# Two feed-forward layers on one core: the first product from a 7-product scheme over 2x2x2 blocks to a 20-product scheme over 3x4x2 blocks

## The chip, the cores and the metric

The kernel runs on one core of a Trainium2 chip. The metric is device microseconds (us) of one execution, lower is better. Engines are named as the profile names them: PE (TensorE), PEld (its weight loads), DVE (VectorE), ACT (ScalarE), POOL (GpSimd), SP (SyncE, which here only issues DMAs).

## The reference

Hashed attention feeds two feed-forward layers. The change is in the layers; of the attention it touches only the last steps, which hand the layers their input.

```
attn_out = attention with a mask of equal hash buckets   # (2, 8, 768, 64)
x = attn_out.transpose(0, 2, 1, 3).reshape(1536, 512)
h = np.maximum(x @ w_in, 0.0);  x = h * h @ w_out        # layer 1, w_in 512x2048, w_out 2048x512
h = x @ w2_in;  out = (h * sigmoid(h)) @ w2_out          # layer 2, same shapes
```

The weights are drawn as float64.

## The kernel before, in words

**Exactness.** Every float32 operand of a product is split into a high part (a cast to fp32r) and a low part (operand minus high part); a product is three matmuls, high-high, high-low, low-high, into one PSUM bank. A 128x512 result with a contraction of 128 is thus three matmuls of 512 columns. Where a value is "cut" below, ACT casts the high part (L158) and DVE or POOL subtracts it (L160); both are in `split` (L156).

**Weights.** They arrive as 64-bit words by DMA, one tile of 128x512 at a time (`convert`, L165), and are rebuilt as float32 by one ACT and four DVE instructions (L173 to L177). A tile of w_in then goes into `wp`, cut on ACT and POOL, four sums of halves are formed on DVE (L215), and these are cut too (`convert_in`, L200); a tile of w_out is cut on ACT and DVE (`convert_out`, L180).

**Loops.** `moe` (L129) runs over two layers m and four ff blocks f; a block has four ff tiles of 128, in two pairs n. Of the 1536 tokens, three token blocks of 512, block 0 is multiplied plainly (`plain`, L220: 4 ff tiles x 4 K tiles x 3 = 48 matmuls, L231). Blocks 1 and 2 go through `quarters` (L253): for each pair n, seven products over two K halves stand for eight (7 x 2 x 3 = 42 matmuls, L260), with five PSUM sums on DVE (L265) and one copy out of PSUM on ACT (L274). The gate is on ACT (`gate`, L244: Relu, and Square at L249, in layer 1; Silu in layer 2), and its result is cut (`gsplit`). `second` (L321) multiplies by w_out, 12 rows of 12 matmuls (L341), and DVE copies (f = 0) or adds (f > 0) each bank into `ys` or `y0` (L352, L355, L361); the last add goes to `ts` and out by DMA. So an ff block has 48 + 84 matmuls in the first product and 144 in the second. `blocks_of_x` (L368) forms the sums of token blocks, once per layer.

**Order.** `Plan` (L53) is a list scheduler that runs when the program is built: each operation is added with its engine, a planned cost, what it reads and writes, and the plan then fixes the order in which each engine's instructions are emitted. PE keeps the order in which its work was added. An operation marked `port` is planned never to run beside a POOL operation. Buffers are handed out in turn: 8 banks, 3 raw weight tiles, 3 float32 weight tiles, 6 scratch tiles `ts`.

**End of the attention.** `wp_put`, `wp_sums`, `x_mul`, `x_put` (POOL) and `t2_t3` (DVE) prepare, among the attention's last steps, the first weights and the token blocks of layer 1.

Of the kernel before, what the change touches and what calls it, by code (L numbers as in the profile page):

```python
# [48 lines left out]
NRAW, NWT, NWO, NTS = 3, 3, 4, 6  # L49
# [3 lines left out]
class Plan:  # L53

# [4 lines left out]
    def add(self, eng, cost, fn, reads=(), writes=(), land=0.0, after=0.0, port=False):  # L63
        n = len(self.ops)
        deps = {self.writer[k] for k in (*reads, *writes) if k in self.writer}
        for k in writes:
            deps.update(self.readers.pop(k, ()))
            self.writer[k] = n
        for k in reads:
            self.readers[k].append(n)  # L70
        if eng == "PE":
            if self.last is not None:
                deps.add(self.last)
            self.last = n
        deps.discard(n)
        self.ops.append((eng, cost, fn, deps, land, after, port or eng == "POOL"))
        return n

    def gap(self, a, b):
        return self.ops[a][4] + (self.lag if self.ops[a][0] != self.ops[b][0] else 0.0)  # L80

    def order(self):
# [6 lines left out]
        for i in reversed(range(n)):  # L89
            tail[i] = ops[i][1] + max((tail[u] + self.gap(i, u) for u in users[i]), default=0.0)  # L90
        left = [len(o[3]) for o in ops]
        when = [o[5] for o in ops]
        ready = defaultdict(list)
        for i in range(n):
            if not left[i]:
                ready[ops[i][0]].append(i)
        begin, port = [0.0] * n, 0.0
        for _ in range(n):
            best = None
            for eng, todo in ready.items():  # L100
                t = self.free.get(eng, 0.0)
                for i in todo:
                    s = max(t, when[i], port if ops[i][6] else 0.0)
                    k = (s, -tail[i], i)
                    if best is None or k < best[0]:
                        best = k, eng, i
            (s, _, _), eng, i = best
            ready[eng].remove(i)
            begin[i] = s
            end = self.free[eng] = s + ops[i][1]  # L110
            if ops[i][6]:
                port = end
            for u in users[i]:
                left[u] -= 1
                when[u] = max(when[u], end + self.gap(i, u))
                if not left[u]:
                    ready[ops[u][0]].append(u)
        self.begin = begin
        return sorted(range(n), key=lambda i: (begin[i], i))

    def emit(self):
        for i in self.order():
            self.ops[i][2]()


STEPS = ("c", "b", "p2", "e", "d", "p4")


def moe(nc, t):  # L129
    mm = nc.tensor.matmul  # L130
    vec, act, gps = nc.vector, nc.scalar, nc.gpsimd
    bank, ts, gq, g0, ys, y0, wp = (t[k] for k in ("bank", "ts", "gq", "g0", "ys", "y0", "wp"))
    plan = Plan(ready={"DVE": 2.6})
    add = plan.add
    count = defaultdict(int)

# [5 lines left out]
    idle = {"bank": list(range(8)), "ts": list(range(NTS))}  # L142

    def new_bank():
        return idle["bank"].pop(0)

    def scratch():
        return idle["ts"].pop(0)

    def done(name, i):  # L150
        idle[name].append(i)

    def tt(eng, cost, op, out, a, b, reads, writes):
        add(("DVE", "POOL")[eng is gps], cost, lambda: eng.tensor_tensor(out=out(), in0=a(), in1=b(), op=op), reads, writes, port=True)

    def split(hi, lo, src, rk, hk, lk, n, pool, after=0.0):  # L156
        h, l = {512: ((0.62, 0.70), (0.62, 1.30)), 1024: ((1.05, 1.28), (1.05, 2.60))}[n][pool]
        add("ACT", h, lambda: act.copy(out=hi(), in_=src()), rk, hk, after=after)  # L158
        eng = gps if pool else vec
        add(("DVE", "POOL")[pool], l, lambda: eng.tensor_tensor(out=lo(), in0=src(), in1=hi().bitcast(F32), op=ALU.subtract), (*rk, *hk), lk, port=True)  # L160
# [4 lines left out]
    def convert(m, io, i):  # L165
        r, w = nxt("raw", NRAW), nxt("wt", NWT)
        rt, wtt = t["raw"][r], t["wt"][w]
        word = rt.bitcast(U32).rearrange("p (n two) -> p n two", two=2)
        hi, lo = word[:, :, 1], word[:, :, 0]
        wu = wtt.bitcast(U32)  # L170
        wk = [("wt", w, 0), ("wt", w, 1)]
        add("SP", 2.9, lambda: nc.sync.dma_start(out=rt, in_=t["src"][m][io][i]), (), [("raw", r)], land=2.5)
        add("ACT", 0.68, lambda: act.activation(out=wtt, in_=hi.bitcast(F32), func=AF.Abs), [("raw", r)], wk)  # L173
        add("DVE", 0.43, lambda: vec.tensor_scalar(out=wtt, in0=wtt, scalar1=W_LO, scalar2=W_HI, op0=ALU.max, op1=ALU.min), wk, wk, port=True)
        add("DVE", 0.43, lambda: vec.tensor_scalar(out=wu, in0=wu, scalar1=5, scalar2=2, op0=ALU.logical_shift_left, op1=ALU.logical_shift_right), wk, wk, port=True)
        add("DVE", 0.70, lambda: vec.scalar_tensor_tensor(out=wu, in0=hi, scalar=0xC0000000, in1=wu, op0=ALU.bitwise_and, op1=ALU.bitwise_or), [("raw", r), *wk], wk, port=True)
        add("DVE", 0.70, lambda: vec.scalar_tensor_tensor(out=wu, in0=lo, scalar=29, in1=wu, op0=ALU.logical_shift_right, op1=ALU.bitwise_or), [("raw", r), *wk], wk, port=True)  # L177
        return w

    def convert_out(m, f):  # L180
        for i in range(FB):
            s = slot[m, f * FB + i] = nxt("wo", NWO)
            if (m, f) == (0, 0) and i < WB:
                r, w = nxt("raw", NRAW), nxt("wt", NWT)
                for cost, fn in t["first"][i]:
                    add("DVE", cost, fn, [("raw", r)], [("wt", w, 0), ("wt", w, 1)], port=True)
            else:
                w = convert(m, 1, f * FB + i)
            hi, lo = t["wo"][s]
            split(lambda h=hi: h, lambda x=lo: x, lambda w=w: t["wt"][w], [("wt", w, 0), ("wt", w, 1)], [("woh", s)], [("wol", s)], 512, False)  # L190

    def put(pb, w, op):
        a = wp[pb]
        src = t["wt"][w].rearrange("p (a b) -> p a b", a=2)
        split(
            lambda: a[:, 0, op : op + 2], lambda: a[:, 1, op : op + 2], lambda: src,
            [("wt", w, 0), ("wt", w, 1)], [("wp", pb, 0, op + k) for k in range(2)], [("wp", pb, 1, op + k) for k in range(2)], 512, True,
        )

    def convert_in(m, f):  # L200
        for n in range(NP):
            pb = n
            w = []
            for h in range(2):
                w.append(convert(m, 0, f * FB + 2 * n + h))
                put(pb, w[h], 2 * h)
            t0, t1 = (t["wt"][x].rearrange("p (a b) -> p a b", a=2) for x in w)
            k = [[("wt", x, j) for j in range(2)] for x in w]
            for out, a, b, op, ko, ka, kb in (
                (t1[:, 1], t1[:, 0], t1[:, 1], ALU.add, k[1][1], k[1][0], k[1][1]),  # L210
                (t1[:, 0], t0[:, 0], t1[:, 0], ALU.subtract, k[1][0], k[0][0], k[1][0]),
# [913 lines left out]
```

## Time and profile before

| | before |
|---|---|
| median of 3 runs (lowest to highest) | 740.61 us (740.59 to 741.18) |
| span of the profiled execution, first to last instruction | 739.4 us |
| instructions | 10895 |
| busy: PE, PEld, DVE, ACT, POOL | 99%, 85%, 83%, 62%, 34% |

The profile gives the profiled execution no other time of its own than its span; the median of the runs is 1.2 us above it. PE and PEld overlap. A matmul's record is longer than the distance to the next one, since matmuls are pipelined; a stretch divided by its number of matmuls gives the pace.

### The profile page before, as it was taken

Reading aid. Unit: us, or ns where it says so; the run is one execution under the profiler, and the core shown is the slowest. Engines: PE = TensorE matmul, PEld = TensorE weight load, DVE = VectorE, ACT = ScalarE, POOL = GpSimd, SP = SyncE. Lnnn points to the kernel's source line nnn. Section 1 sums busy time; section 2 is a strip of 40 time slices with the busy share of each in tenths; the row PEclk is TensorE's granted clock in tenths of the full one; section 3 lists DMA queues with packets and bytes.
Section 4 is the critical chain, followed back from the end, with each engine's and each line's share of the span. In section 5 each row is a group of like instructions: output and inputs, shape, how many; then the busy total and the mean of one; then the engine's idle time right before and its main releaser. Section 6 shows DMA issues by size and latency. Waiting matters only on the chain.

```text
span 739.4 us, 10895 instructions
## 1 busy us (share of the span) xinstructions
PE 732.1 (99%) x3734; PEld 627.3 (85%) x3735; DVE 610.0 (83%) x1152; ACT 461.6 (62%) x866; POOL 249.6 (34%) x219
## 2 busy tenths in 40 slices
PE   8999999999999999999999999999999999999998
PEld 4799999999998888888888888888888888888887
DVE  6899999999999998887878896788888777776442
ACT  7888998998896882773566278366335525623510
POOL 7547477877674104103103103500330320230000
PEclk9999999999999999999999999999999999999999
DMA  6987787686462113311320220002133024010012
GB/s 180 210 175 151 182 186 176 154 186 148 115 157 60 57 60 111 114 59 57 114 86 24 91 86 28 29 28 87 58 99 129 30 78 150 1 58 1 1 71 100
DMA packets 27687, 71.87 MB, mean 97 GB/s; under 512 B 4208, under 2 KB 9120, under 8 KB 27632
## 3 DMA queue, kind: packets, MB, share of 16 engines
q1 hardware_dynamic: 24872, 64.52, 31.4%
q0 software_dynamic: 2160, 5.90, 3.9%
q10 hardware_dynamic: 600, 0.75, 0.4%
q8 instruction: 30, 0.49, 0.3%
q14 instruction: 25, 0.20, 0.1%
HBM read 49.80 MB, written 3.15 MB: 72 GB/s over the span
## 4 chain that ended last, share of the span: by engine, by line
PE 95%; DVE 2%; DMA 2%; ACT 1%; issue 0%; SPq 0%; DVEq 0%; ACTq 0%
PE bank L341 35%; PE bank L260 21%; PE bank L231 12%; PE s L741 8%; PE t L777 8%; PE o L802 4%; PE o L801 4%; PE bt L534 1%; DMA fr<-in_dram 1%; PE bs L534 1%; DMA kk<-bt 1%; PE rb L831 1%; DVE tl L788 1%; DVE mt L748 1%; ACT P L761 0%
## 5 line engine op out<-in xcount | busy, mean ns | idle before, releaser
L160 POOL TENSOR_TENSOR wp<-wt,wp 128x512 fp32r<-128x512 f32 x56 | 78.2, 1407 | 329.5 <-ACT wp L158 307.5
L260 PE MATMUL bank<-xb,wp 128*128 128x512 f32 x480 | 110.1, 389 | 0.0
L788 DVE TENSOR_TENSOR tl<-t,th 128x384 fp32r<-128x384 f32 x192 | 104.8, 548 | 2.4 <-ACT th L782 2.2
L260 PEld LDWEIGHTS bank<-xb,wp 128*128 128x128 f32 x480 | 90.1, 188 | 18.7
L761 ACT ACTIVATE P<-s,mt 128x768 f32<-128x768 f32 x96 | 95.6, 996 | 10.6 <-DVE mt L753 7.1
L748 DVE TENSOR_REDUCE mt<-s 128x1 f32<-128x768 f32 x96 | 91.4, 952 | 5.5 <-PE s L741 4.9
L741 PE MATMUL s<-kk,qq 76*128 76x384 f32 (+1 forms) x384 | 84.5, 341 | 1.6 <-DMA kk<-bt 0.8
L782 ACT CAST th<-t 128x384 fp32r<-128x384 f32 x192 | 82.2, 483 | 4.0 <-PE t L777 3.4
L158 ACT CAST wp<-wt 128x512 fp32r<-128x512 f32 x56 | 34.2, 619 | 78.2 <-DVE wt L215 44.5
L231 PE MATMUL bank<-x0h,wp 128*128 128x512 f32 x256 | 80.2, 389 | 0.0
L777 PE MATMUL t<-ident,P 128*128 128x128 f32 x576 | 79.1, 272 | 1.0 <-DVE tl L788 0.9
L777 PEld LDWEIGHTS t<-ident,P 128*128 128x128 f32 x576 | 67.8, 140 | 5.7 <-DVE tl L788 1.1
L801 PE MATMUL o<-th,vv 128*128 128x384 f32 x192 | 72.5, 377 | 0.0
L741 PEld LDWEIGHTS s<-kk,qq 76*128 76x128 f32 (+1 forms) x384 | 67.8, 188 | 4.3 <-ACT P L761 2.1
L265 DVE TENSOR_TENSOR ts<-bank,ts 128x512 f32<-128x512 f32 x80 | 54.4, 690 | 19.8 <-PE bank L260 17.2
L802 PE MATMUL o<-tl,vv 128*128 128x384 f32 x192 | 64.5, 336 | 0.2 <-DVE tl L788 0.2
L245 ACT ACTIVATE ts<-bank 128x512 f32<-128x512 f32 x48 | 28.6, 596 | 49.4 <-PE bank L260 28.9
L231 PEld LDWEIGHTS bank<-x0h,wp 128*128 128x128 f32 x256 | 48.1, 188 | 9.9
L160 DVE TENSOR_TENSOR gql<-ts,gqh 128x512 fp32r<-128x512 f32 x64 | 43.8, 703 | 8.9 <-ACT gqh L158 8.9
L173 ACT ACTIVATE wt<-raw 128x512 f32<-128x512 f32 x58 | 38.1, 671 | 20.2 <-POOL wp L160 17.6
L341 PE MATMUL bank<-wol,gqh 128*128 128x512 f32 (+1 forms) x132 | 50.5, 383 | 0.0
L341 PE MATMUL bank<-woh,gql 128*128 128x512 f32 (+1 forms) x132 | 50.5, 383 | 0.0
(185 smaller groups left out, 1631.7 us busy)
## 6 DMA issues: line engine op xcount, KB each, us to landing
raw<-in_dram SPq DMA_DIRECT2D x64, 512.0 KB
kk<-in_dram POOLq DMA_DIRECT2D x15, 384.0 KB, 6.1
qq<-hq SPq DMA_DIRECT2D x28, 192.0 KB
vr<-in_dram SPq DMA_DIRECT2D x8, 384.0 KB
ta<-ob SPq DMA_DIRECT2D x31, 96.0 KB
tb<-ob SPq DMA_DIRECT2D x31, 96.0 KB
out_dram<-ts SPq DMA_DIRECT2D x11, 256.0 KB
rq<-in_dram SPq DMA_DIRECT2D x7, 384.0 KB
```

The source lines that it names most:

```text
L160: add(("DVE", "POOL")[pool], l, lambda: eng.tensor_tensor(out=lo(), in0=src(), in1=hi().bitcast(F32), op=ALU.subtract), (*rk, *hk), lk, po ...
L231: mm(bank[b], w[:, x, op, sl], t["x0"][y][:, kt], start=kt == 0 and j == 0, stop=kt == 3 and j == 2)
L260: mm(bank[b], w[:, p, op, k * 128 : k * 128 + 128], x[:, q, xop, k], start=first and k == 0 and j == 0, stop=k == 1 and j == 2, skip_group ...
L341: mm(bank[b][:, 0:wd], x, y, start=i == 0 and n == 0, stop=i == FB - 1 and n == 2)
L741: mm(s[:, n, 0:QW], t["qq"][h][0:kk, ab, c0 : c0 + 128], t["kk"][h][0:kk, ab, n * QW : (n + 1) * QW], start=ab == 0, stop=ab == 1)
L748: nc.vector.tensor_reduce(out=m[:, 0:1], in_=s[:, :, 0:QW], op=ALU.max, axis=AX.XY, negate=True)
L761: nc.scalar.activation(out=e.rearrange("p (a b) -> p a b", a=2), in_=s[:, :, 0:QW], func=AF.Exp, scale=m[:, 1:2], bias=m[:, 2:3], accum_ou ...
L777: nc.tensor.transpose(t[:, j * 128 : (j + 1) * 128], P[u, j][:, kt * 128 : (kt + 1) * 128], ident)
L782: nc.scalar.copy(out=th, in_=PT[g][0][:, 0:QW])
L788: nc.vector.tensor_tensor(out=tl, in0=t[:, 0:QW], in1=th.bitcast(F32), op=ALU.subtract)
L801: mm(o[:, 0:QW], vv, th, start=kt == 0, stop=False)
L802: mm(o[:, 0:QW], vv, tl, start=False, stop=kt == KT - 1)
```

## The change

The first product of both layers now runs over all three token blocks at once.

- In the first ff block of a layer (f = 0) it is plain for all three token blocks (3 x 48 = 144 matmuls). In the other three, `fast` multiplies, for each pair n, 3 token blocks x 4 K tiles x 2 ff tiles with 20 products of three matmuls in place of 24: 2 x 20 x 3 = 120 matmuls.
- The 20 products accumulate in chains (`CHAIN`): A and B each run on in one bank while partial results are read out between products; C and D are single products; K10, K20 and F are banks that DVE first fills ("seeds") with a sum, and on which PE then accumulates with `start=False`. Per pair n there are ten DVE instructions that read PSUM (seven into SBUF, three into another bank) and three ACT copies out of PSUM.
- Operands: eight x operands live in `xk`, twelve in `xw`; `operands()` forms them in the f = 0 block by 16 sums and 12 cuts, in place in `yf`, the one 128x4x1536 tile that holds x and later y. Weight operands: `convert_in(m, f, n)` now loads two tiles, rebuilds both with 1024-wide instructions in the one buffer `both`, forms 8 sums (one of 512, five of 256, two of 128 columns) in four groups, and cuts five groups of four 128-column tiles into `wpa` and `wpb`.
- Scratch, gate results and sums are 25 cells of 2 KB, handed out in turn (`Cell`). The 12 gate results of a block hold 24 of them until `second` is done with their token block. There are 2 raw weight tiles in place of 3.
- `second`: in layer 1 for every other row, in layer 2 for all rows but the last, ACT copies the old y into the bank first, PE accumulates on it, and DVE or ACT copies the bank out; else DVE adds as before. The order of token blocks is 1, 0, 2 (0, 1, 2 in the first block of all), and for the first of them the first two ff tiles of all four rows come before the last two. `convert_in` of the next block is added before the first and the second token block.
- `Plan` may give SBUF sums and cuts to DVE or POOL, and bank copies to DVE or ACT, whichever ends first in its plan.
- In the attention, `wp_sums`, four of eight `wp_put` and `t2_t3` go, `x_put` cuts token block 0 for four and blocks 1 and 2 for two pairs, and does one copy or sum less each.

The diff, cut to its core:

```diff
-NRAW, NWT, NWO, NTS = 3, 3, 4, 6
+NRAW, NWO, NCELL = 2, 4, 25
...
+CHAIN = {"A": (1, 2, 5, 7, 9, 15, 20), "B": (3, 4, 6, 11, 14, 16), "C": (8,), "D": (10,), "K10": (12, 18), "K20": (13, 17), "F": (19,)}
+ORDER = (8, 3, 1, 4, 2, 6, 12, 18, 11, 5, 14, 16, 7, 10, 13, 9, 17, 19, 15, 20)
+WPA = (12, 17, 6, 7, 14, 15, 11, 9)
+WPB = (18, 16, 8, 20, 13, 3, 19, 2, 4, 5, 10, 1)
+TURN = (1, 0, 2)
+SEED = [[r % 2 for r in range(NT // 128)], [1] * (NT // 128)]
...
+    EITHER = {128: (0.2, 0.45), 256: (0.35, 0.75), 512: (0.62, 1.3), 1024: (1.05, 2.6)}
...
+    def cut(hi, lo, src, rk, hk, lk, pool=True, after=0.0):
+        add("ACT", 0.62, lambda: act.copy(out=val(hi), in_=val(src)), rk, hk, after=after)
+        tt(ALU.subtract, lo, src, lambda: val(hi).bitcast(F32), 512, (*rk, *hk), lk, pool)
+
+    def psum(out, b, other, reads, writes):
+        add("DVE", 0.70, lambda: vec.tensor_tensor(out=val(out), in0=bank[b], in1=val(other), op=ALU.add), [("bank", b), *reads], writes)
...
+        for g, parts in enumerate(groups):
+            s = Cell()
+            for a, b, x, y, op in parts:
...
+                tt(op, out, x, y, 128 * (b - a), wk, [s.key])
+            o = (wpa, wpb)[g // 2][n][:, :, g % 2 * 4 : g % 2 * 4 + 4]
+            cut(o[:, 0], o[:, 1], lambda s=s: s().rearrange("p (b c) -> p b c", c=128), [s.key], [("wp", n, g, 0)], [("wp", n, g, 1)])
+            s.free()
...
+                for z, (p, q) in enumerate(((0, 0), (0, 1), (1, 0))):
+                    mm(bank[b], w[:, p], x[:, q], start=not started and z == 0, stop=z == 2, skip_group_check=started)
+
+            add("PE", 0.68, go, [*wkeys(n, r), *(("xo", r, q) for q in range(2))], [("bank", b)])
+            after(n, r, at, temp[n])
...
+        for r in order:
+            for n in range(NP):
+                product(n, r)
...
+            start = f == 0 or final or not SEED[m][r]
+            if not start:
+                add("ACT", 0.55, lambda src=src, yt=yt: act.copy(out=src, in_=yt), [yk], [("bank", b)])
...
+                fast(m, ORDER)
+            for k, c in enumerate(((0, 1, 2), TURN)[m] if f == 0 else TURN):
+                if k < NP and not (m == 1 and f == NFB - 1):
+                    convert_in(m + turn, (f + 1) % NFB, k)
+                second(m, f, c, k == 0)
...
-        def t2_t3(k):
...
```

## Rows read from the trace of the kernel before

**Rows 1.** The page: span, PE's busy time, the chain's shares by engine.

```profile
span 739.4 us, 10895 instructions
...
PE 732.1 (99%) x3734; PEld 627.3 (85%) x3735; DVE 610.0 (83%) x1152; ACT 461.6 (62%) x866; POOL 249.6 (34%) x219
...
PE 95%; DVE 2%; DMA 2%; ACT 1%; issue 0%; SPq 0%; DVEq 0%; ACTq 0%
```

**Rows 2.** The chain in order of time: start, length, work; one ff block, the end.

```profile
360.77 10.88 PE bank L231 x48
371.65 19.04 PE bank L260 x84
390.69 32.64 PE bank L341 x144
...
703.50 32.80 PE bank L341 x156
```

**Rows 3.** Stretches: us; PE, PEld, DVE, ACT, POOL busy (x instructions); PEclk; DMA; GB/s.

```profile
235.40:736.30 500.90, 500.88 (x2223) 415.21 (x2220) 386.91 (x619) 253.63 (x420) 88.66 (x61) 1.00 0.20 67
360.77:423.33 62.56, 62.56 (x278) 51.82 (x277) 50.15 (x81) 35.67 (x61) 11.21 (x8) 1.00 0.25 84
578.38:640.93 62.55, 62.55 (x277) 51.81 (x277) 47.10 (x81) 29.16 (x50) 12.81 (x10) 1.00 0.23 76
```

**Rows 4.** Instruction groups of DVE: count, busy us, mean ns of one.

```profile
L265 DVE TENSOR_TENSOR ts<-bank,ts 128x512 f32<-128x512 f32 x80 | 54.4, 690 | 19.8 <-PE bank L260 17.2
L160 DVE TENSOR_TENSOR gql<-ts,gqh 128x512 fp32r<-128x512 f32 x64 | 43.8, 703 | 8.9 <-ACT gqh L158 8.9
L215 DVE TENSOR_TENSOR wt<-wt,wt 128x256 f32<-128x256 f32 x28 | 13.2, 470 | 0.8
L176 DVE SCALAR_TENSOR_TENSOR wt<-raw,wt 128x512 uint32<-128x512 uint32 x58 | 46.9, 811 | 1.3
L177 DVE SCALAR_TENSOR_TENSOR wt<-raw,wt 128x512 uint32<-128x512 uint32 x58 | 40.6, 710 | 0.7
L174 DVE TENSOR_SCALAR wt<-wt 128x512 f32<-128x512 f32 x58 | 28.3, 487 | 2.9 <-ACT wt L173 2.8
L175 DVE TENSOR_SCALAR wt<-wt 128x512 uint32<-128x512 uint32 x58 | 27.2, 469 | 1.5
L154 DVE TENSOR_TENSOR ys<-ys 128x1024 f32<-128x1024 f32 x5 | 6.1, 1217 | 0.0
```

**Rows 5.** Instruction groups of ACT, same columns.

```profile
L158 ACT CAST wp<-wt 128x512 fp32r<-128x512 f32 x56 | 34.2, 619 | 78.2 <-DVE wt L215 44.5 <-DVE wt L177 33.8
L249 ACT ACTIVATE ts<-ts 128x512 f32<-128x512 f32 x48 | 30.3, 632 | 1.2
L274 ACT COPY ts<-bank 128x512 f32<-128x512 f32 x16 | 9.4, 586 | 11.2 <-PE bank L260 10.8
```

**Rows 6.** The low parts of the weights on POOL, same columns.

```profile
L160 POOL TENSOR_TENSOR wp<-wt,wp 128x512 fp32r<-128x512 f32 x56 | 78.2, 1407 | 329.5 <-ACT wp L158 307.5 <-issue 21.7 <-POOL wp L160 0.4
```

**Rows 7.** Timeline of DVE: start, length, instruction, idle time before it.

```profile
332.10 0.68 DVE L160 TENSOR_TENSOR gql<-ts,gqh 128x512 fp32r<-128x512 f32 x1
332.70 0.68 DVE L177 SCALAR_TENSOR_TENSOR wt<-raw,wt 128x512 uint32<-128x512 uint32 x1
333.61 0.69 DVE L355 TENSOR_TENSOR y<-bank,y 128x512 f32<-128x512 f32 x1 [0.23 <-PE bank L341]
```

**Rows 8.** Timeline of POOL about 299 us.

```profile
298.95 1.74 POOL L160 TENSOR_TENSOR wp<-wt,wp 128x512 fp32r<-128x512 f32 x1 [1.01 <-ACT wp L158]
```

**Rows 9.** Timeline of DVE about 299 us.

```profile
299.49 1.48 DVE L174 TENSOR_SCALAR wt<-wt 128x512 f32<-128x512 f32 x1
301.43 0.43 DVE L174 TENSOR_SCALAR wt<-wt 128x512 f32<-128x512 f32 x1
```

**Rows 10.** Timeline where the attention ends and the layers begin.

```profile
235.35 1.38 DVE L991 TENSOR_TENSOR ys<-ys 128x512 f32<-128x512 f32 x1
235.40 0.48 PE L231 MATMUL bank<-x0h,wp 128*128 128x512 f32 x1
```

More of the change, by code (lines that the diff above doesn't have):

```diff
@@ L140, in nxt @@
         return i
[L142 to L160, printed above, removed]
@@ new lines, in tt, with go @@
+    def tt(op, out, a, b, n, reads, writes, pool=True, after=0.0):
+        d, p = EITHER[n]
+        def go(eng):
+            ENG[eng].tensor_tensor(out=val(out), in0=val(a), in1=val(b), op=op)
+        add((("DVE", d), ("POOL", p)) if pool else "DVE", d, go if pool else partial(go, "DVE"), reads, writes, after=after, port=True)
+    def cut(hi, lo, src, rk, hk, lk, pool=True, after=0.0):
+        add("ACT", 0.62, lambda: act.copy(out=val(hi), in_=val(src)), rk, hk, after=after)
+        tt(ALU.subtract, lo, src, lambda: val(hi).bitcast(F32), 512, (*rk, *hk), lk, pool)
@@ L190, in convert_out @@
[L190 to L197, printed above, removed]
-        )
@@ L200, in convert_in @@
[L200 to L211, printed above, removed]
-                (t0[:, 0], t1[:, 1], t0[:, 0], ALU.subtract, k[0][0], k[1][1], k[0][0]),
-                (t0[:, 1], t0[:, 1], t0[:, 0], ALU.subtract, k[0][1], k[0][1], k[0][0]),
-            ):
-                add("DVE", 0.45, lambda out=out, a=a, b=b, op=op: vec.tensor_tensor(out=out, in0=a, in1=b, op=op), [ka, kb], [ko], port=True)
-            for h in range(2):
-                put(pb, w[h], 4 + 2 * h)
@@ new lines, in wkeys, with xo, block, gate @@
+    def wkeys(n, r):
+        part, i = WAT[r]
+        return [("wp", n, 2 * part + i // 4, x) for x in range(2)]
+    def xo(r):
+        part, i = XAT[r]
+        return (xk, xw)[part][:, :, i]
+    def block(i, j):
+        return yf[:, j, i * CH : (i + 1) * CH]
+    gs = {}
+    def gate(m, n, c, b=None, cell=None):
+        g = cell or Cell()
+        src, key = (g, g.key) if b is None else (lambda: bank[b], ("bank", b))
+        add("ACT", 0.62, lambda: act.activation(out=g(), in_=src(), func=AF.Silu if m else AF.Relu), [key], [g.key])
+        if m == 0:
+            add("ACT", 0.63, lambda: act.activation(out=g(), in_=g(), func=AF.Square), [g.key], [g.key])
+        hi, lo = gs[n, c] = Cell(F32R), Cell(F32R)
+        cut(hi, lo, g, [g.key], [hi.key], [lo.key])
+        g.free()
@@ new lines, in second, with x_cut, single, x_op @@
+        for z in ((0, 2), (2, 4)) if split else ((0, 4),):
+            for part, finish in jobs:
+                for i in range(*z):
+                    part(i)
+                if z[1] == FB:
+                    finish()
+    def x_cut(r, src, key, after=0.0):
+        x = xo(r)
+        cut(x[:, 0], x[:, 1], src, [key], [("xo", r, 0)], [("xo", r, 1)], after=after)
+    def single(i, j, after=0.0):
+        x_cut(AT[i, j], block(i, j), ("yf", i, j), after)
+    def x_op(out, a, op, b):
+        tt(ALU.add if op == "+" else ALU.subtract, block(*out), block(*a), block(*b), 512, [("yf", *a), ("yf", *b)], [("yf", *out)])
```

577 lines of the change are left out of this document (291 added, 286 removed).

## The prediction

> **What bounds the kernel now.** I read the page first: PE is busy for 732.1 of 739.4 us, and 95% of the chain that ended last is PE [rows 1]. Whether PE waits inside the layers is seen in the stretches: from the first product of layer 1 to the last matmul of layer 2 it is busy for 500.88 of 500.90 us, at a granted clock of 1.00, 2.4 GHz [rows 3]. The chain in order of time says what a matmul costs there: 48 in 10.88 us, 84 in 19.04, 144 in 32.64, all 0.2267 us each [rows 2]. So an ff block is 276 matmuls and 62.56 us, nothing else is on the path, and the end is 3.1 us after the last matmul (703.50 + 32.80 to 739.4) [rows 1, 2]. Beside PE, DVE is the fullest engine: 50.15 of 62.56 us in a block of layer 1, 47.10 in one of layer 2; ACT and POOL have room [rows 3].
>
> **What goes from PE.** The first product falls from 8 x 132 = 1056 matmuls to 2 x 144 + 6 x 120 = 1008; the second product keeps its number. 48 x 0.2267 = **10.9 us** less, if PE never waits. By blocks: +2.7 us in the two f = 0 blocks (65.3 us), -2.7 in the other six (59.84 us).
>
> **What comes onto DVE.** I count a block with f > 0 of layer 1 by record lengths [rows 4]. First the block of before, as a test: 8 weight tiles x (0.487 + 0.469 + 0.811 + 0.710 = 2.48) = 19.8; 8 half sums x 0.47 = 3.8; 16 low parts x 0.70 = 11.2; 10 sums and 12 adds out of PSUM x 0.69 = 15.2; together 50.0, against 50.15 in [rows 3]. Now the changed block. Four w_out tiles: 9.9. Two pairs of w_in tiles, 1024 wide: a 1024-wide operation took 1.217, or 1.73 times the 0.70 of a 512-wide one, so 2 x 1.73 x 2.48 = 8.6 (bounds 8.6 and 9.9, twice as long). Sums of weights per pair: 0.70 + 5 x 0.47, and two of 128 columns, unseen, between half of 0.47 and all of it, I take 0.33: 3.7, for two pairs 7.4. Low parts: 4 + 10 + 12 = 26 x 0.70 = 18.3, if all stay on DVE (the ten of w_in were on POOL). Out of PSUM: 20 x 0.69 = 13.8, and 6 adds 4.1. The six of these that write another bank have no row; nearest are 0.69 and, above, the longest 512-wide one, 0.81; I take 0.69. Together **62.1 us** against PE's 59.84; in layer 2, with no adds and the copies on ACT, 57.9.
>
> The records overstate it: in [rows 7] DVE starts a 0.68 instruction 0.60 after the one before. By that pace, 0.88 of the records, the block needs 54.7 us (91% of PE's time) in layer 1 and 51.0 (85%) in layer 2. I go by the pace, since it is what a full queue does. In an f = 0 block the count is 18.5 for weights, 7.4 sums, 18.3 low parts and 28 operations for the operands (19.6): 63.8 of 65.3 by records, 56.1 by pace.
>
> **What POOL can take.** In [rows 8, 9] a DVE instruction of 0.43 us that starts while POOL subtracts lasts 1.48, to 0.28 after POOL's end: 1.05 us lost for one POOL operation. A low part handed over frees 0.70 on DVE and costs POOL 1.41 [rows 6], so it relieves DVE only while DVE works out of PSUM. The Trainium skill (SBUF — State Buffer, "SBUF: two separate sides") says the same: the port pair that DVE and GpSimd share is locked for a whole instruction and the loser blocks. By that rule, with which the 1.48 agrees, handing work over does not shrink the 62.1; without it, six low parts on POOL would bring it under 59.84.
>
> **ACT and the rest.** Per block ACT gets four more copies out of PSUM (0.59), two more cuts (0.62), 6 to 12 bank seeds and as many copies [rows 5]. Writing PSUM has no row; between 0.59 and 0.62, I take 0.6. That makes some 46 us in either layer, under 59.84: hidden. Two raw tiles in place of three: the loads of one pair begin when the other has been rebuilt, and run beside its sums; hidden, else they lengthen the weights' path below. In f = 0, y may overwrite `yf` only after the operands have read it, but eight banks let `second` run 8 x 2.72 = 21.8 us without a copy, so the operands' 19.6 us have 32.6 + 21.8: hidden. Where the attention ends, the first product starts at 235.40, 0.05 after a `t2_t3` instruction that goes on for 1.38 [rows 10]: it doesn't wait for it, so DVE's four and POOL's fewer operations there are worth 0 (at best some 0.4 us). Tail: same last row, same add, 3.1 us.
>
> **New waits.** In `fast` a bank of chain A or B is read, then accumulated on again three products later: 3 x 0.68 = 2.04 us, of which the read takes 0.69 and which an idle DVE starts as soon as the bank is done, like the add in the last row of [rows 7]. Some 1.3 us remain, nearly two other DVE instructions. Behind a late read stands PE itself. Nothing like that existed at this tightness (before, four products of 1.36). I price it, with DVE at 91%, at **1.5 us** for the whole kernel; bounds are 0 (PE's waits now) and 6.8 (next part).
>
> **Sum.** 739.4 - 10.9 + 1.5 = 730.0 us of span; the median stands 1.2 above the span, so **731.2 us**. Its own range is 729.3 (no wait, 0.4 gained in the attention) to 734.
>
> **The rivals.**
> - **DVE becomes the bound of layer 1.** If records count and not the pace, three blocks take 62.1 and not 59.84: 3 x 2.3 = 6.8 back, 736.5; with the wide rebuild at 9.9, 3 x 3.6 = 10.7, 740.4. For: DVE's windows equal my count by records. Against: the pace of [rows 7]; and that count holds the waits behind 11.21 us of POOL, which need not come again.
> - **Hand-offs slip.** One more late read of about 0.7 to 1 us in each `fast`: 6 us, 735.7. For: ten reads per pair at 2.04 us. Against: an idle DVE takes a finished bank at once [rows 7], and at 91% it is often idle.
> - **Weights come late: slower.** Of 25 cells 24 hold gate results when `convert_in` of pair 0 forms its sums, so its four groups go one by one through one cell, and `both` is one buffer for both pairs. After the last product: gate, square, cast, low part 0.59 + 0.63 + 0.62 + 0.70 = 2.5; four groups, sums 3.7 and 4 x (0.62 + 0.70), reach 11.5; pair 1 may be rebuilt from 10.2, ACT 1.2 and DVE 4.3 end at 15.7; its sums, five low parts and a cast at 23.5. PE wants them after its 32.64 us of second product [rows 2, 4, 5]. But DVE also has there six adds 4.1, three last gates 2.1, two w_out tiles 5.0: if all go first, 34.7, and with two of the serial low parts on POOL 36.1. That is 3.5 late, in six blocks 21 us: 740.6 - 10.9 + 21 = 750.7. It decides from 1.8 us late (10.9 / 6), so from 34.4. For: one cell, one buffer. Against: 9 us of slack if the chain goes first, which the plan's order by remaining path favours.
>
> **How the numbers follow.** Forecast 0.58, hand-offs 0.08, DVE bound 0.17 (0.10 of it under 739.1, 0.06 about equal, 0.01 above), weights late 0.17 (0.02 about equal, 0.15 slower). A measurement tells 0.2%, 1.5 us, from no change. Faster: 0.58 + 0.08 + 0.10 = 0.76; same 0.08; slower 0.16. The range takes in all but the late weights: 729.3 to 740.5.
>
> **What would show it.** Right: PE in the layers again without idle time but a microsecond or two, in some 490 to 491.5 us; 120 matmuls in 27.2 us; DVE at 54 to 57 us of a 59.8 us block in layer 1. DVE bound: blocks of layer 1 longer than 60 us with DVE without gaps, those of layer 2 not. Hand-offs: PE waiting in `fast` for the DVE sums or seeds, about half a microsecond at a time. Late weights: one PE wait of microseconds at the head of each `fast`, for the low parts of `wpb`. Wrong altogether would be a longer pace than 0.2267 per matmul, or a wait at the f = 0 blocks, which I put at nothing.

## The result, and the profile after

The changed kernel takes **733.38 us** (median of 4 runs, 732.89 to 733.72) against 740.74 us (4 runs, 740.59 to 741.18) before on the same chip: a ratio of 0.9903 (95% interval 0.9889 to 0.9917), 7.4 us faster. The forecast was 731.2 us, 9.5 us less than these 740.74; the range of 729.3 to 740.5 holds the time. The profiled execution took 733.29 us for a span of 731.5 us.

The page after: span, busy times, shares of the chain by engine, as in [rows 1].

```profile
span 731.5 us, 10921 instructions
...
PE 722.8 (99%) x3687; PEld 617.9 (84%) x3687; DVE 637.1 (87%) x1209; ACT 530.9 (73%) x1011; POOL 187.0 (26%) x165
...
PE 92%; DVE 5%; DMA 2%; ACT 1%; issue 0%; DVEq 0%; POOL 0%; ACTq 0%
```

PE's share of the chain fell from 95% to 92%, DVE's rose from 2% to 5%: some of the end is now set by DVE. The windows of both layers, of the f = 0 block of layer 1 and of its three other blocks, and of the first two `fast` blocks of layer 2 show where; columns as in [rows 3].

```profile
235.09:728.36 493.27, 491.52 (x2173) 405.36 (x2171) 414.66 (x677) 323.21 (x564) 42.50 (x29) 1.00 0.19 68
235.09:300.39 65.30, 65.30 (x290) 54.08 (x289) 56.13 (x91) 44.78 (x76) 3.60 (x3) 1.00 0.18 65
300.39:360.93 60.54, 60.16 (x266) 49.43 (x265) 52.80 (x90) 41.20 (x74) 4.13 (x3) 1.00 0.18 64
360.93:422.08 61.15, 60.42 (x265) 49.38 (x265) 54.52 (x93) 41.31 (x73) 4.12 (x3) 1.00 0.20 72
422.08:482.72 60.64, 60.41 (x265) 49.40 (x265) 54.04 (x81) 42.75 (x76) 12.70 (x8) 1.00 0.16 55
...
548.00:608.52 60.52, 60.13 (x265) 49.48 (x265) 53.84 (x91) 39.87 (x71) 8.49 (x6) 1.00 0.20 70
608.52:668.36 59.84, 59.84 (x265) 49.55 (x265) 51.38 (x88) 40.46 (x71) 2.60 (x2) 1.00 0.20 71
```

A block without waits is 65.28 or 59.84 us at the pace of [rows 2], and the two layers are 489.8 (2 x 65.28 + 6 x 59.84, and 0.16 for the last matmuls). They take 493.27, so PE waits 3.5 us; that is 1.8 us over the 490 to 491.5 us that the prediction named for the layers. The waits are in four blocks, three of layer 1 and one of layer 2. DVE stands at 53 to 55 us in the blocks of layer 1, not at 60. The granted clock is 1.00 throughout, 2.4 GHz.

The chain in order of time says at which point of a block PE waits.

```profile
304.85 23.42 PE bank L325 x102
328.27 32.65 PE bank L432 x144
...
362.14 1.29 DVE wpb L182 x2
363.44 1.22 DVE wpa L182 x2
...
364.74 0.10 DVE cell L191
...
366.03 0.61 DVE cell L191
...
366.69 22.75 PE bank L325 x99
...
608.52 27.20 PE bank L325 x120
```

Without waits a `fast` is 27.20 us, as at 608.52; after 328.27 comes 32.65 us of second product, as before. The `fast` that begins at 360.93 is broken within its first seven products: PE runs on from 366.69 when DVE has read bank B (L191). Before that read DVE was subtracting low parts of the new weights. The waits of PEld in the layers say the same:

```profile
PEld bank L325 <- DVE cell L191: 4.3, 6, 0.9
```

All six of these waits are for the same read, that of bank B after product 3, of either pair. PEld's waits sum to 4.3 us; what PE lost is read from the stretches. The lengths of the six `fast` stretches are 27.88, 28.51, 28.00, 27.88, 27.20 and 27.20 us, 3.5 us over. DVE's timeline shows the queue in front of the read, and the place where it came from.

```profile
342.13 1.48 DVE L182 TENSOR_TENSOR cell<-cell,cell 128x512 fp32r<-128x512 f32 x2
343.64 0.69 DVE L182 TENSOR_TENSOR cell<-both 128x512 f32<-128x512 f32 x1
...
360.56 1.36 DVE L182 TENSOR_TENSOR cell<-both 128x512 f32<-128x512 f32 x3
362.14 0.69 DVE L182 TENSOR_TENSOR wpb<-cell,wpb 128x512 fp32r<-128x512 f32 x1 [0.23 <-ACT wpb L187]
362.75 0.68 DVE L182 TENSOR_TENSOR wpb<-both,wpb 128x512 fp32r<-128x512 f32 x1
363.36 1.28 DVE L182 TENSOR_TENSOR wpa<-cell,wpa 128x512 fp32r<-128x512 f32 x2
364.74 0.69 DVE L191 TENSOR_TENSOR cell<-bank,cell 128x512 f32<-128x512 f32 x1
365.35 0.68 DVE L447 TENSOR_TENSOR yf<-bank,yf 128x512 f32<-128x512 f32 x1
365.95 1.28 DVE L191 TENSOR_TENSOR cell<-bank,cell 128x512 f32<-128x512 f32 x2
```

The first sum of pair 0 starts at 343.64, right behind the last low part of a gate result, 15.4 us into the second product that began at 328.27. The last low part of pair 1 ends at 364.64, 3.7 us after the second product has ended; an add of the old y (L447) stands between the reads of the two pairs. PE doesn't wait for the weights (it needs the groups one by one, and each is there in time), but the bank that PE needs again is read only when DVE has come through them. ACT's timeline says why the gate results were late:

```profile
328.11 1.06 ACT L285 ACTIVATE cell<-bank 128x512 f32<-128x512 f32 x2
...
337.25 0.58 ACT L285 ACTIVATE cell<-bank 128x512 f32<-128x512 f32 x1
...
338.77 1.13 ACT L187 CAST cell<-cell 128x512 fp32r<-128x512 f32 x2
```

A gate takes three ACT instructions (L285, L287, L187); `fast` finishes its last banks close together, and ACT is at their gates until 339.9. At the head of the two first `fast` of a layer the queue in front of the read holds low parts of the x operands (`xw`) too, and in layer 2 copies of y out of a bank (L443). The costs of single operations, by group:

```profile
L191 DVE TENSOR_TENSOR bank<-bank,cell 128x512 f32<-128x512 f32 x36 | 24.4, 695 | 2.9 <-PE bank L325 2.9
L182 DVE TENSOR_TENSOR cell<-both 128x128 f32<-128x128 f32 x24 | 5.8, 286 | 0.0
...
L417 ACT COPY bank<-yf 128x512 f32<-128x512 f32 x53 | 30.7, 587 | 1.9 <-DVE cell L191 1.2
```

### The profile page after: what moved, and what is told of

It reads as the page before. It is cut to its first block, busy times and chain, and to the rows that moved or that the text cites. A ratio compares the mean times of both kernels' runs of the same rounds, so it can differ in the third digit from the quotient of the medians.

```text
span 731.5 us, 10921 instructions
## 1 busy us (share of the span) xinstructions
PE 722.8 (99%) x3687; PEld 617.9 (84%) x3687; DVE 637.1 (87%) x1209; ACT 530.9 (73%) x1011; POOL 187.0 (26%) x165
## 4 chain that ended last, share of the span: by engine, by line
PE 92%; DVE 5%; DMA 2%; ACT 1%; issue 0%; DVEq 0%; POOL 0%; ACTq 0%
PE bank L432 32%; PE bank L325 21%; PE s L812 9%; PE bank L302 9%; PE t L848 8%; PE o L873 4%; PE o L872 4%; DMA kk<-in_dram 1%; PE bs L615 1%; PE bt L615 1%; DVE wpb L182 1%; DVE cell L182 1%; DVE xw L182 1%; PE rb L902 1%; DVE yf L182 1%
## 5 line engine op out<-in xcount | busy, mean ns | idle before, releaser
L432 PE MATMUL bank<-woh,cell 128*128 128x512 f32 (+1 forms) x392 | 119.3, 385 | 0.0
L432 PE MATMUL bank<-cell,woh 128*128 128x512 f32 x384 | 118.2, 389 | 0.0
L432 PEld LDWEIGHTS bank<-woh,cell 128*128 128x128 f32 x392 | 73.1, 188 | 14.7
L432 PEld LDWEIGHTS bank<-cell,woh 128*128 128x128 f32 x384 | 72.1, 188 | 14.9
L432 PE MATMUL bank<-wol,cell 128*128 128x512 f32 (+1 forms) x196 | 75.4, 385 | 0.0
L432 PE MATMUL bank<-cell,wol 128*128 128x512 f32 x192 | 74.7, 389 | 0.0
L285 ACT ACTIVATE cell<-bank 128x512 f32<-128x512 f32 x72 | 42.6, 593 | 43.2 <-PE bank L325 32.6
L325 PE MATMUL bank<-xw,wpb 128*128 128x512 f32 x288 | 71.9, 392 | 1.7 <-DVE cell L191 1.7
L182 DVE TENSOR_TENSOR cell<-cell,cell 128x512 fp32r<-128x512 f32 x79 | 54.6, 701 | 17.1 <-ACT cell L187 16.6
L325 PEld LDWEIGHTS bank<-xw,wpb 128*128 128x128 f32 x288 | 53.6, 188 | 15.1 <-DVE cell L191 4.3
```

The lines of the kernel that those rows point to most:

```text
L182: ENG[eng].tensor_tensor(out=val(out), in0=val(a), in1=val(b), op=op)
L325: mm(bank[b], w[:, p], x[:, q], start=not started and z == 0, stop=z == 2, skip_group_check=started)
L432: mm(bank[b][:, 0:wd], x, y, start=start and i == 0 and z == 0, stop=i == FB - 1 and z == 2, skip_group_check=not start)
```

## The experiments

Two theories of the 3.5 us stood at first. One: bank hand-offs are tight by themselves, so any DVE instruction ahead of a read costs. The other: the weights' chain starts late, because one free cell, one `both` and two raw tiles hold it up, and the read of bank B only shows it. PE's waits are given here as the length of both layers less 489.8 us. Every edit also lets the planner choose a new order for all engines; so a run shows what an edit and its new order do together.

**ACT reads bank B.** The first read of bank B becomes an ACT copy, and the sum is made from SBUF.

```diff
-                into(T, "20", at["B"], "00")
+                keep(T, "20", at["B"])
+                y, x = T["00"], T["20"]
+                tt(ALU.add, x, x, y, 512, [x.key, y.key], [x.key])
```

> Edit: after product 3 ACT copies bank B into the cell, and DVE or POOL adds the other cell later from SBUF; DVE no longer stands between products 3 and 4. Measured by how much longer than 490.0 us PE takes from its first product in layer 1 to its last matmul (changed kernel: 493.3, so 3.3 us of waits, at the head of four of the six 20-product stretches, all for the DVE read of bank B). Theory hand-off (DVE is still at weights and operands when that read is due, and only the read holds PE): the waits at product 4 go; what is left is at most half, as the next DVE read is due 2.7 us later: 490.0 to 491.7. Rival weights (PE would have had to wait for the low parts of the weights anyhow): the waits move to the matmuls that use wpb and wpa, total within 0.7 us of 493.3.

740.11 us (one run, beside 740.35 before); the layers take 499.90 us, 10.1 us of waits. It was expected to help or to do nothing, and both theories missed: the waits moved to later reads of banks, most of them behind DVE again, some behind the ACT copies.

```profile
PEld bank L325 <- DVE cell L191: 9.8, 12, 1.5
PEld bank L325 <- ACT cell L332: 2.0, 2, 1.3
```

The planner also laid 44 instead of 29 POOL operations into the layers. DVE's timeline of this kernel shows what stood before one of the late reads:

```profile
316.49 1.42 DVE L211 TENSOR_SCALAR cell<-cell 128x512 f32<-128x512 f32 x1
317.95 1.40 DVE L212 TENSOR_SCALAR cell<-cell 128x512 uint32<-128x512 uint32 x1
319.38 1.66 DVE L213 SCALAR_TENSOR_TENSOR cell<-raw,cell 128x512 uint32<-128x512 uint32 x1
320.96 2.47 DVE L191 TENSOR_TENSOR cell<-bank,cell 128x512 f32<-128x512 f32 x4
```

and POOL's, at the same time:

```profile
316.33 1.29 POOL L182 TENSOR_TENSOR wol<-cell,woh 128x512 fp32r<-128x512 f32 x1 [5.55 <-ACT woh L187]
317.58 2.90 POOL L182 TENSOR_TENSOR cell<-cell,cell 128x512 fp32r<-128x512 f32 x2
```

The three DVE instructions, otherwise 0.42, 0.46 and 0.69 us, each last 1 us longer while POOL works: the effect of [rows 8, 9], now ahead of a bank that PE wants.

**Two more cells.** 27 cells in place of 25; for the room, operand 14 is written into 18's place. So the kernel leaves out one operand and doesn't compute the layers; PE has as many matmuls as before.

```diff
-NRAW, NWO, NCELL = 2, 4, 25
+NRAW, NWO, NCELL = 2, 4, 27
...
-MADE = (16, 5, 15, 7, 1, 2, 3, 4, 6, 13, 14, 18)
+MADE = (16, 5, 15, 7, 1, 2, 3, 4, 6, 13, 18)
...
+XAT[14] = XAT[18]
```

> Edit: 27 cells in place of 25; the room comes from writing operand 14 into the place of operand 18, so the products that read either use the later one. So the sums of pair 0's weights go through three cells in turn, not one. Theory one cell (the serial groups make the preparation end some 4 us after the second product ends): preparation ends 3 us or more earlier, PE's waits fall from 3.3 us to under 1: first product to last matmul 490.0 to 491. Rival raw tiles (the preparation is late because the rebuild of pair 0 starts 8.8 us into the second product, when its two raw tiles have been freed and loaded): the rebuild still starts there, the chain gets shorter by at most 1 to 2 us, waits stay at 2 to 3.3 us.

729.34 us (one run, beside 740.35). The layers, same columns as above:

```profile
234.49:724.29 489.80, 489.79 (x2173) 405.82 (x2171) 407.99 (x674) 324.46 (x568) 38.17 (x28) 1.00 0.20 69
```

No wait is left. The second product before the second `fast` begins at 327.01 here and ends at 359.65; the first sums of pair 0 run at 341.35, 14.3 us into it (15.4 in the changed kernel), and the sums of several groups go one after another, not one group at a time. At the head of the second `fast` DVE does this:

```profile
360.61 0.68 DVE L183 TENSOR_TENSOR wpa<-cell,wpa 128x512 fp32r<-128x512 f32 x1
361.80 0.69 DVE L192 TENSOR_TENSOR cell<-bank,cell 128x512 f32<-128x512 f32 x1 [0.51 <-PE bank L326]
362.40 0.68 DVE L183 TENSOR_TENSOR wpa<-cell,wpa 128x512 fp32r<-128x512 f32 x1
363.00 0.68 DVE L192 TENSOR_TENSOR cell<-bank,cell 128x512 f32<-128x512 f32 x1
```

The last low part of pair 1 ends at 363.08, 3.4 us after the second product, hardly earlier than in the changed kernel (3.7). But the low parts in front of the first read of bank B end at 361.29, 1.6 us after it, so DVE is idle when the bank is done, and the last low part stands between the two reads. What took the wait away here is that the work in front of the read ends 2 us earlier, not that the weights do.

**Two more raw tiles.** Four raw weight tiles, for whose room operands 17 and 20 are written into the places of 19 and 11; 25 cells as in the change. Here two operands are left out, and again the layers aren't computed.

```diff
-NRAW, NWO, NCELL = 2, 4, 25
+NRAW, NWO, NCELL = 4, 4, 25
...
-KEPT = (19, 11, 8, 9, 12, 10, 17, 20)
+KEPT = (19, 11, 8, 9, 12, 10)
...
+XAT[17], XAT[20] = XAT[19], XAT[11]
```

> Edit: 4 raw tiles in place of 2; the room comes from writing operands 17 and 20 into the places of 19 and 11, so the products that read these use the wrong one of the two. Theory raw tiles: the rebuild of pair 0 starts before the second product or at its head (in the changed kernel 8.8 us in), pair 1's weights are done 4 us or more before the 20 products begin, and PE's waits fall from 3.3 us to under 1: 490.0 to 491. Rival one cell: pair 0's sums cannot begin before the last gate in any case and go one by one, so waits fall by no more than half: 491.6 to 493.3.

738.18 us (one run). The layers begin late, at 237.65 (234.4 to 235.7 in the other runs): the granted clock was 0.86 in the first 20 us of the program, a mean of its two levels of 1.2 and 2.4 GHz, where the changed kernel had 1.00. The layers take 495.58, 5.8 us of waits, 2.3 more than the change's, and both expectations missed. The rebuild of pair 0 does run earlier: from 0.8 us before the second product (331.92) to 4.7 us into it, against 8.8 to 12.7 us in the changed kernel. Its first sum runs at 344.96, 13.0 us into the second product (15.4 in the changed kernel), behind the last low part of a gate as before. But the planner also gave POOL 41 operations, so this run alone doesn't say what raw tiles are worth; the last experiment says more.

**One product moved.** Product 17, the last of its bank, before product 9, so that the gates of this bank start two products (1.36 us) earlier.

```diff
-ORDER = (8, 3, 1, 4, 2, 6, 12, 18, 11, 5, 14, 16, 7, 10, 13, 9, 17, 19, 15, 20)
+ORDER = (8, 3, 1, 4, 2, 6, 12, 18, 11, 5, 14, 16, 7, 10, 13, 17, 9, 19, 15, 20)
```

> Edit: only the order of the products: 17 (both pairs) before 9. The bank K20 and its gate come 1.36 us earlier, bank A's read and its gate later. Theory hand-off: the gates at the end of the stretch and with them the first steps of the preparation move by about 1 us, the queue at the head of the next stretch gets shorter by that, and each of the four waits of 0.6 to 1.3 us falls by up to 1 us: 490.3 to 492. Rival weights or raw tiles: the raw tiles are freed at the same place, nothing changes: 492.8 to 493.6.

731.86 us (one run, beside 740.35); the layers take 491.95, 2.2 us of waits, as the hand-off theory had it. The waits at the heads of the second and third `fast` fall from 1.3 and 0.8 us to 0.2 each, those at the first `fast` of each layer stay (0.7 and 1.0 us). Whether it is the earlier gates is not shown: before the second `fast` the first sum of pair 0 starts 14.6 us into the second product in place of 15.4, but before the third 15.2 in place of 15.4; and in both the two reads of bank B now stand side by side on DVE, with the add of y behind them.

**The weights after the first token block.** `convert_in` of both pairs is added behind the second product of the first token block, when nine cells are free.

```diff
-                if k < NP and not (m == 1 and f == NFB - 1):
-                    convert_in(m + turn, (f + 1) % NFB, k)
                 second(m, f, c, k == 0)
+                if not (m == 1 and f == NFB - 1):
+                    for n in range(NP) if k == 0 else ():
+                        convert_in(m + turn, (f + 1) % NFB, n)
```

> Edit: the weights of the next block are added to the plan after the second product of the first token block instead of before it, so that the sums of both pairs find nine free cells (the first block's gate results are done) instead of one; 25 cells, same result as the reference. Theory one cell: as with 27 cells, PE's waits go, first product to last matmul 489.8 to 490.5, and the time is 3 us under the changed kernel's 733.4: 729.5 to 730.7. Rival (with 27 cells it was the dropped operand place, or the weights are late whatever the cells): the sums start later, waits of 0.6 to 1.3 us stay at the head of four or more stretches, 732.5 to 735.

733.01 us (4 runs, 732.81 to 733.30; before 740.09, 7 runs): ratio 0.9906 (0.9890 to 0.9923), the same as the change, so the expected 729.5 to 730.7 was missed. The layers take 493.47, 3.7 us of waits, but at other places. The waits at the heads of the second and third `fast`, 2.1 us in the change, are gone. A new one, 1.42 us, is in the middle of the second `fast`, on DVE:

```profile
373.88 1.38 DVE L191 TENSOR_TENSOR bank<-bank,cell 128x512 f32<-128x512 f32 x2 [1.71 <-PE bank L325]
375.17 1.44 DVE L211 TENSOR_SCALAR cell<-cell 128x512 f32<-128x512 f32 x1
376.64 1.40 DVE L212 TENSOR_SCALAR cell<-cell 128x512 uint32<-128x512 uint32 x1
378.07 1.67 DVE L213 SCALAR_TENSOR_TENSOR cell<-raw,cell 128x512 uint32<-128x512 uint32 x1
379.66 2.47 DVE L191 TENSOR_TENSOR cell<-bank,cell 128x512 f32<-128x512 f32 x4
```

It is the pattern of the first experiment: three weight instructions beside POOL (three instructions, from 375.02 to 379.18) take 4.5 us in place of 1.6, and PE resumes at 380.39 with the read. The others, 1.39 and 0.87 us, are at the heads of the first `fast` of each layer (0.68 each in the change), where low parts of the x operands and a copy of y stand in front of the read beside those of the weights.

**No POOL in the layers.** Sums and low parts go to DVE alone.

```diff
-        add((("DVE", d), ("POOL", p)) if pool else "DVE", d, go if pool else partial(go, "DVE"), reads, writes, after=after, port=True)
+        add("DVE", d, partial(go, "DVE"), reads, writes, after=after, port=True)
```

> Edit: POOL gets no sum and no cut in the layers; the 28 it had go to DVE. Theory lock: each of these took as much from DVE by making it wait as it spared, so DVE's busy time in the layers stays at 414.7 us, give or take 8, and PE's waits stay at 2.5 to 5 us. Rival (POOL's help is what keeps DVE under PE): DVE rises by 28 x 0.6 = 17 us to 432, and waits grow to 6 us or more.

732.01 us (one run, beside 740.09); the layers take 492.48, 2.7 us of waits. DVE has 422.7 us in the layers, 8 more for 28 operations more, between the two expectations' 414.7 and 432, and PE waits less, not more. The waits at the first `fast` of each layer are gone (27.24 and 27.22 us); the two that are left are at the head of the second and third `fast` of layer 1, 1.3 us each, where low parts of the weights and the add of y stand in front of the reads.

**POOL free to run beside DVE.** The planner no longer keeps DVE's SBUF work and POOL's apart.

```diff
-                if ops[i][6] or e == "POOL":
-                    s = max(s, port)
```

> Edit: the plan no longer keeps POOL's operations apart from those DVE operations that work from and to SBUF, so it hands POOL some 97 sums and cuts in the layers instead of 28. Theory lock (a DVE instruction that works from SBUF waits for POOL's to end, as the 1.48 us for a 0.43 us instruction showed): DVE's total busy time in the layers (414.7 us) does not fall by the 70 x 0.6 = 42 us handed over, but stays above 400 us, and PE waits as much or more than in the changed kernel: 493 to 500 us from first product to last matmul. Rival (POOL works beside DVE): DVE falls to some 375 us, the queue is never full, waits vanish: 490 to 491.

751.77 us (one run, beside 740.09). POOL takes 98 operations, and DVE is none the lighter; the window holds some matmuls' length on either side of the layers:

```profile
234.00:747.00 513.00, 498.18 (x2179) 408.89 (x2177) 435.26 (x612) 320.33 (x562) 138.01 (x98) 0.99 0.19 66
```

65 instructions fewer on DVE than in the change (612 against 677), and 20.6 us more busy time. That DVE gets nothing out of POOL was expected with the lock; that the layers would take 512.3 us (234.51 to 746.82), 22.5 more than without waits, was not. Some 3 us of these are the first `fast` of layer 2, at a mean granted clock of 0.89 (before it PE had been busy for 16.4 of 20.6 us); most of the rest are waits. The plan that ran here was made as if DVE and POOL didn't slow each other, so its order is part of what it costs.

**The adds of y back on DVE in layer 2.** No bank of layer 2 is seeded with the old y, so DVE adds it.

```diff
-SEED = [[r % 2 for r in range(NT // 128)], [1] * (NT // 128)]
+SEED = [[r % 2 for r in range(NT // 128)], [0] * (NT // 128)]
```

> Edit: in layer 2 no bank is seeded; DVE adds the old y to every bank, 12 adds of 0.69 us a block, as before the change, and ACT loses its 24 copies. Theory one cell plus a full DVE queue: as in layer 1, these adds stand between the serial steps of the weights, so the second and third 20-product stretches of layer 2, which had no wait, get waits of 0.6 to 1.3 us each; first product to last matmul 494.0 to 496. Rival (DVE's load beside the chain does not matter, layer 1 waits for its own reasons such as the Square of its gate): layer 2 stays without waits there, 493.3 give or take 0.3.

733.94 us (one run, beside 740.09); the layers take 494.32, 4.5 us of waits. DVE has 431.5 us in place of 414.7, 17 us more, and PE waits 1 us more: the second and third `fast` of layer 2, 27.20 us in the change, become 27.64 and 27.70. The time is in the range of the first theory, the place is not: these two waits are in the middle of `fast`, where DVE rebuilds w_out tiles, a step of it stretched to 1.66 us and two of their low parts to 2.38 beside POOL. The heads of these two `fast` stay without a wait, so the adds are not what sets layer 1 apart there. What does was not tested; layer 2's gate has no Square, and in the changed kernel the last low part ends there 33.8 us after the start of the second product (635.72), in layer 1 36.4 us. The length of DVE's work costs PE little; what PE pays for is what stands in front of a read when a bank is done.

**Weights after the first token block, and no POOL.** The two edits together, since either had taken away the other's cause.

> Edit: the weights' sums after the first token block (nine free cells) and no POOL work in the layers, both together; same result as the reference. Theory two causes (one cell, and DVE instructions from SBUF that wait for POOL just ahead of a bank read): neither wait is left but for the head of the first 20-product stretch of a layer, where operands stand in the queue; first product to last matmul 489.8 to 491.5, time 729.5 to 731. Rival (DVE is too full: POOL's 28 to 41 operations are needed): waits of 0.5 us or more in most stretches, 492.5 or more, 732.5 or more.

**729.23 us** (5 runs, 729.11 to 729.99; before 740.68, 9 runs, 739.98 to 743.87): ratio 0.9847 (0.9831 to 0.9863), faster than either kernel (the change's interval is 0.9889 to 0.9917). The first two `fast` in the chain, and DVE at the head of the first:

```profile
300.08 27.20 PE bank L325 x120
...
359.92 27.20 PE bank L325 x120
```

```profile
302.72 1.28 DVE L191 TENSOR_TENSOR cell<-bank,cell 128x512 f32<-128x512 f32 x2
303.92 0.69 DVE L182 TENSOR_TENSOR wpa<-cell,wpa 128x512 fp32r<-128x512 f32 x1
```

All six `fast` are 27.20 us and nothing but PE is in the chain of the layers. Each edit alone left waits (3.7 and 2.7 us), together none: the late weights and POOL can each put time in front of a read. That POOL is enough for a wait by itself doesn't follow: with 27 cells it kept 28 operations, and no wait was left. Nor do late weights by themselves make one: in the first `fast` here the last low part ends at 304.61, 4.5 us after the second product, later than anywhere in the changed kernel, but behind the two reads, and PE doesn't wait.

**Banks read after one product.** On top of the last kernel, the kernel's other order, in which banks are read and accumulated on again with less between.

```diff
-                fast(m, ORDER)
+                fast(m, EARLY)
```

> Edit: on top of the two above, the other order of products (8, 3, 4, 6, 11, 14, 1, 2, ...): chain B's bank is read and accumulated on again after one product (0.68 us) instead of three (2.04 us). Theory hand-off (the read of 0.69 us on DVE or 0.59 on ACT must fit between): each of some eight such steps per stretch costs PE 0.3 to 1 us, 3 to 6 us a stretch, 18 to 36 us over six: 508 to 526 us from first product to last matmul. Rival (an idle DVE hides it, since the read of one pair runs while PE is at the other pair): under 1 us a stretch, below 496.

750.28 us (one run, beside 740.68); the layers take 509.6, as expected with the hand-off; 19.8 us of waits, 2.6 to 3.9 in a `fast`.

```profile
PEld bank L325 <- DVE cell L191: 15.3, 29, 1.3
PEld bank L325 <- ACT cell L332: 7.2, 18, 1.0
PEld bank L325 <- DVE bank L191: 3.8, 7, 0.7
```

With the same work on DVE and none on POOL, the order with shorter distances between a bank's read and its next product makes 20 us. The three products of the change's order are not slack, they are what the hand-offs cost.

**Two more raw tiles, no POOL.** The third experiment without its 41 POOL operations: four raw tiles, with two operands left out for them, 25 cells, `convert_in` in its old place, nothing on POOL.

> Edit: 4 raw tiles as before (operands 17 and 20 written into the places of 19 and 11), one cell as in the changed kernel, and no POOL work in the layers, so that POOL's waits don't hide what the raw tiles do. Theory one cell (free only when the last of the gates has gone through ACT, some 14 us into the second product): the rebuild of pair 0 starts early but its sums don't; waits of 0.5 to 1.3 us stay at the heads in layer 1: 491.5 to 493. Rival raw tiles: waits under 0.7 us in all: 489.8 to 490.5.

730.33 us (one run, beside 740.68); the layers take 490.64, 0.8 us of waits, where two raw tiles left 2.7. The result lies between the two expectations. The first sum of pair 0 runs at 339.59 here, 12.4 us into the second product, against 15.0 with two raw tiles and no POOL (342.04 for 327.07): the rebuild is over earlier, and so are the last gates' low parts on DVE. With POOL out, the raw tiles are, by this one run, a second hold on the weights' chain beside the one cell.

## Why the prediction held, and which terms were off

**PE's products: right.** 120 matmuls take 27.20 us and an f = 0 block 65.30; the 10.9 us are there in full.

**DVE's load: right by the pace.** Said were 56.1 us for an f = 0 block, 54.7 and 51.0 for the others of layer 1 and 2; measured are 56.1 for that of layer 1, 52.8 to 54.5, and 51.4 in the block of layer 2 shown without a wait (53.8 in the one with). Layer 2's f = 0 block has 58.6. POOL took some of it; in the ninth experiment, with all of it on DVE, blocks with f > 0 hold 54.1 to 56.1 us in layer 1 and 54.1 to 55.2 in layer 2, where DVE also makes three to seven copies of y a block that the forecast gave to ACT. The rival "DVE becomes the bound" falls: 17 us more on DVE in layer 2 cost 1 us. The unseen prices: 695 ns for a DVE sum into a bank (0.69 said), 587 for an ACT copy into one (0.6), 286 for 128 columns (0.33). The four DVE steps of a pair's rebuild take 3.9 us (4.3 said). ACT needs 40 to 43 us in a block with f > 0 (46 said).

**POOL: right in the main.** That "handing work over does not shrink the 62.1" was half so: in the sixth experiment the 28 operations come back to DVE and its busy time rises by 8 us, where 28 x 0.60 by the pace are 17; in the seventh, 69 more on POOL raise it by 20.6. That a POOL operation can hurt, when a bank read stands behind the DVE instruction that it stretches, wasn't said. In the changed kernel it has a part in the waits at the first `fast` of each layer, which go when POOL has no work; the fifth experiment, where it is 1.4 us at once, shows it best. The rule of the Trainium skill (SBUF — State Buffer, "SBUF: two separate sides") says that the loser blocks for the whole instruction; the 1.0 us by which each of three instructions grew beside POOL agrees.

**New waits: the term that was mis-sized.** "I price it, with DVE at 91%, at **1.5 us** for the whole kernel": it is 3.5, inside the bounds of 0 and 6.8. The 1.5 was set between its bounds without a working, so that it came this near is in part luck. The place was the one named, a bank read by DVE and wanted again three products later, and the sign is the one that the prediction gave for "hand-offs slip": PE waits in `fast` for DVE sums, by its records 0.2 to 0.5 us at a time. The cause was not general tightness, though. What stands in front of the read comes from the rival "weights come late", at a small part of its price, and two steps of that rival failed:
- "After the last product: gate, square, cast, low part 0.59 + 0.63 + 0.62 + 0.70 = 2.5" prices one gate. Some gates of the last products queue on ACT until 339.9, and the cell is free 15.4 us into the second product, 13 us later than that. So the good end, 23.5 us, was never near: the chain ended 36.4 us after the last product (328.27 to 364.64), about the bad end of 36.1.
- "That is 3.5 late, in six blocks 21 us" took PE to need all the weights at the head of `fast`. It needs them group by group, so what 36.4 us cost is what the read of bank B stands behind the last low parts: 0.7 to 1.3 us, in four blocks of six. With two more cells and the same order of products the last low part still ends 36.1 us after the last product, but fewer stand in front of the read, and all of the wait was gone.

"Hand-offs slip" as it was priced (one late read in each `fast`, 6 us) is not what happened: the late reads are at four heads only, and for the reason above; the tenth experiment shows how much it would be with a shorter distance.

**The f = 0 blocks: nearly right.** Their length has no wait in it. But "the operands' 19.6 us have 32.6 + 21.8: hidden" was not quite so: the last of their low parts (`xw`, at 303.50) stands in the queue before the first read of bank B, and is part of the 0.7 us of the first `fast` of layer 1; in layer 2 a sum and copies of y stand there.

**The attention and the offset: they cancel, by luck.** PE's timeline has the first product at 234.85 in place of 235.40 [rows 10]; the forecast was 0 to 0.4. The times of the runs after are some 1.8 us above their spans, and so are those of the runs of the kernel before that were timed beside the experiments (740.35 for a span of 738.6), so the 1.2 of the forecast compared the span of one execution with the median of others. By terms of the span: 739.4 - 10.9 + 3.5 - 0.55 = 731.45, against 731.5; then 1.9 to the median of 733.38. The layers begin at 234.4 to 235.7 us from one run to the next at full clock, so the 0.55 is as likely a difference of executions as a gain; it wasn't tested.

Not tried: one more cell with no operand left out for it, sums formed in place in the weights' low parts, and, the plainest test of the account above, a plan that differs only in putting the first reads of bank B ahead of the last low parts. What made the planner's order worse when ACT reads bank B is only partly shown: POOL's stretching of DVE stands before one of the late reads in the trace, the others weren't followed.

## What to carry to other kernels

When PE has no slack, the price of preparing operands is not their sum but what stands in the queue before an instruction that PE waits for: find, at the head of each stretch, the first bank read that PE needs back, and count what DVE does before it. A scratch pool that is full for a moment delays work by the time in which it empties, which goes by the engine that empties it (here ACT's gates), not by the length of one item. A helper engine that slows its neighbour is best left out where that neighbour's next instruction is one that PE waits for. Test two suspected causes together as well as one by one: here the later weights alone gained nothing, no POOL alone 0.8 us in the layers, and both together all 3.5.

## What the runs showed of the hardware that was not expected

- Removing all 28 POOL operations from the layers raised DVE's busy time by 8 us and made the layers 0.8 us shorter (492.48 against 493.27); 69 more of them raised it by 20.6 us and made the kernel 18 us slower (751.77 against 733.38), some 3 us of it a stretch at a lower granted clock. These are one run each; of the three amounts of POOL work, none at all was the best.
- A bank seeded by ACT costs what a copy out of a bank costs (587 against 586 ns in [rows 5]), and a DVE sum from bank to bank 695 ns, hardly more than one into SBUF (685 here, 690 in [rows 4]).
